# Running the first two groups of a gated-linear-attention + MLP kernel as pairs of units, in the order in which rows and weights land, with x transposed on TensorE and v cast by the software DMA queue

## Chip, cores, metric

One core of a Trainium2 chip (trn2). The metric is the device time of one execution in microseconds, the median of several runs.

## The reference, cut to what matters

```python
# q, k, v, alpha: (B=4, H=8, S=768, D=48), float32
for t in range(S):                      # a gated recurrence, per batch and head
    state = alpha[:, :, t, :, None] * state + einsum('bhd,bhe->bhde', k[:, :, t], v[:, :, t])
    y[:, :, t] = einsum('bhd,bhde->bhe', q[:, :, t], state)
x = y.transpose(0, 2, 1, 3).reshape(3072, 384)
out = gelu_tanh(x @ w_in) @ w_out       # w_in 384 x 2048, w_out 2048 x 384
```

The kernel cuts the sequence into six chunks of 128 rows. A *unit* is one chunk of one batch; a *group* is one chunk of all four batches (four units), a *pair* is two units of a group.

## The kernel before

For each pair: Ln of alpha on ScalarE (`e_ln`), a running sum by a matmul with a triangle (`e_cum`), Exp of it and of its negative and the products with q and k on VectorE (`e_exp`). For each unit: transposes of the scaled q and k on TensorE and their eviction (`t_qk`), the masked scores (`attn`), the new state (`kv`), and the output y, cast to x (`y`). A DMA transpose turns x into xT. Layer 1 then takes a whole group: 16 pieces of 3 matmuls of 512 columns, each with a gelu. Layer 2 has 64 matmuls of 384 columns a group. The *software queue* is that of the DMAs which GpSimd issues, the *hardware queue* that of the DMAs which SyncE issues. A *table load* is ScalarE's exchange of its function tables, which it makes before a Ln, an Exp or a gelu whose set is not loaded (1.28 us each in these traces).

```python
    def load(self, n, group, part=None, cast=False):
        ...
        nc.gpsimd.dma_start(t[:, lo:hi]..., src)              # every load by the software queue
    def cast_v(self, group, part, eng):                       # v of group 0: loaded float32, cast by an engine
        eng(self.loaded["vb", c][:, sl], self.loaded["v", c][:, sl])

    def y(self, cb, xT, i):
        ...
        nc.scalar.copy(x, yps...)
        nc.sync.dma_start_transpose(xT[:, :, i, :], x)        # x to xT by DMA

    def run(self):
        # loads, all from GpSimd: a q k of pair 0, a of pair 1, v of pair 0, q k of pair 1, w_in[0],
        # v of pair 1, w_in[1..3], a q k (by pairs) and v of group 1, w_out[0..3]
        ...
        for i, p in enumerate(pairs[0]):
            ln[i](); cum[i](); exp[i]()
            for cb in p: self.t_qk(cb, nc.scalar.copy)
            self.cast_v(G[0], i, nc.gpsimd.tensor_copy if i == 0 else nc.scalar.copy)
            for cb in p: self.attn(cb)
            for j, cb in enumerate(p): self.yk(cb, xT0, 2 * i + j)
        # then: layer 1 of group 0; Ln, Exp and scores of group 1 with nothing beside them;
        # layer 2 of group g-1 merged with kv, y of group g and Ln, Exp of group g+1;
        # layer 1 of group g merged with the scores of group g+1; and so on to layer 2 of group 5
```

Of the kernel before, what the change touches and what calls it, by code (L numbers as in the profile page):

```python
# [13 lines left out]
DMA_X = True  # L14
# [25 lines left out]
class _Kernel:  # L40
# [41 lines left out]
    def load(self, n, group, part=None, cast=False):  # L82

        nc, C, H, D = self.nc, self.C, self.H, self.D
        c = group[0][0]
        key = (n, c)
        if key not in self.loaded:
            if n == "v" and not cast:
                self.loaded[key] = self.ld.tile([C, len(group), H, D], F32, tag="v32", bufs=1, name="v32")
            else:  # L90
                self.loaded[key] = self.ld.tile([C, len(group), H, D], BF16 if n == "v" else F32, tag=n,
                                                bufs=3 if n == "v" else 2, name=n)
        t = self.loaded[key]
        lo, hi = (0, len(group)) if part is None else (2 * part, 2 * part + 2)
        src = self.src[n][lo:hi].rearrange("b h s d -> s (b h) d")[c * C:(c + 1) * C]
        nc.gpsimd.dma_start(t[:, lo:hi].rearrange("t b h d -> t (b h) d"), src)  # L96
        if n == "v" and cast:
            self.set_v(group, t)
        elif n != "v":
            for i in range(lo, hi, 2):  # L100
                self.u.setdefault(group[i], {})[n + "pair"] = t[:, i:i + 2]

    def set_v(self, group, t):
        for i, cb in enumerate(group):
            self.u.setdefault(cb, {})["v"] = t[:, i]

    def cast_v(self, group, part, eng):
        c = group[0][0]
        if ("vb", c) not in self.loaded:
            t = self.loaded["vb", c] = self.ld.tile([self.C, len(group), self.H, self.D], BF16, tag="v", bufs=3,  # L110
                                                    name="v")
            self.set_v(group, t)
        sl = slice(2 * part, 2 * part + 2)
        eng(self.loaded["vb", c][:, sl], self.loaded["v", c][:, sl])  # L114
# [109 lines left out]
    def y(self, cb, xT, i):  # L224
# [14 lines left out]
        if DMA_X:  # L239
            nc.sync.dma_start_transpose(xT[:, :, i, :], x)  # L240
        else:
            ps = self.ps.tile([C, self.NKT, C], BF16, tag="yk", bufs=2, name="xT_ps")
            for j in range(self.NKT):
                nc.tensor.transpose(ps[:, j, :], x[:, j * C:(j + 1) * C], self.ident)
            nc.vector.tensor_copy(xT[:, :, i, :], ps)
        del self.u[cb]


    def layer1(self, xT, gT):
        nc, C, N = self.nc, self.C, xT.shape[2]  # L250

        def piece(nt):
            h = self.ps.tile([C, N * C], F32, tag="ff", bufs=4, name="hT")
            for j in range(self.NKT):
                nc.tensor.matmul(h, self.w_in[:, j, nt * C:(nt + 1) * C],  # L255
                                 xT[:, j].rearrange("p g t -> p (g t)"),
                                 start=j == 0, stop=j == self.NKT - 1)
            nc.scalar.activation(gT[:, nt, :], h, AF.Gelu_apprx_tanh)  # L258
# [3 lines left out]
    def layer2(self, group, gT, by_part=False):  # L262
# [16 lines left out]
        if by_part:  # L279
            return [lambda mt=mt, part=part: piece(mt, part)  # L280
                    for part in range(self.NFT // 4) for mt in range(len(group))]
        return [lambda mt=mt, part=part: piece(mt, part)
                for mt in range(len(group)) for part in range(self.NFT // 4)]


    def run(self):
# [3 lines left out]
        self.load("a", G[0], 0)  # L290
        make_upper_triangular(nc, self.ut_h, val=1.0, diag=True)
# [5 lines left out]
        self.load("q", G[0], 0)  # L297
        self.load("k", G[0], 0)
        make_identity(nc, self.ident)
        self.load("a", G[0], 1)  # L300
        self.load("v", G[0], 0)
        self.load("q", G[0], 1)
        self.load("k", G[0], 1)
        self.load_w_in(0)
        self.load("v", G[0], 1)
        for i in (1, 2, 3):
            self.load_w_in(i)
        self.load("a", G[1], 0)
        self.load("q", G[1], 0)
        self.load("k", G[1], 0)  # L310
        self.load("a", G[1], 1)
        self.load("q", G[1], 1)
        self.load("k", G[1], 1)
        self.load("v", G[1], cast=True)
        for i in range(4):
            self.load_w_out(i)
        for b in range(self.B):
            for i in range(2):
                nc.vector.memset(self.state[b][i], 0.0)

        def decays(pp):
            return ([lambda p=p: self.e_ln(p) for p in pp],
                    [lambda p=p: self.e_cum(p) for p in pp],
                    [lambda p=p: self.e_exp(p) for p in pp])

        ln, cum, exp = decays(pairs[0])
        xT0 = self.grp.tile([self.C, self.NKT, 4, self.C], BF16, tag="xT", name="xT")
        for i, p in enumerate(pairs[0]):
            ln[i]()
            cum[i]()  # L330
            exp[i]()
            for cb in p:
                self.t_qk(cb, nc.scalar.copy)
# [85 lines left out]
```

## Time and profile before

| | before |
|---|---|
| time, median of the first 3 runs | 253.8 us (253.43 to 255.75) |
| span of the profiled run | 254.0 us |
| busy: TensorE, ScalarE, VectorE, GpSimd | 71%, 47%, 41%, 21% |
| layer 1 of group 0, 1, 2 starts at | 66.7, 115, 144.8 us |

The busy shares are averages over two stages that are limited by different things, so the last row is of more use: a change in the first two groups is worth what it takes from 144.8 us, as long as the steady rest keeps its length. The lines of the profile that carry this stand in the prediction.

In these lines PE is TensorE, PEld its weight loads, ACT ScalarE, DVE VectorE, POOL GpSimd, SP SyncE; L255 is a line of the kernel; hT is the result of layer 1, gT its gelu, acc the sum of layer 2, ot the output tile. A line of the chain of waits gives start, length (us) and what; a line of the list of waits gives the engine that waits, what it waits for, the total, the times and the longest wait. Slices are counted from 0.

### The profile page before, as it was taken

How to read it: one execution, taken by the hardware profiler on the slowest of the kernel's cores; microseconds unless marked ns; L12 is line 12 of the kernel's file. 1: busy time of each engine (PE TensorE's matmuls, PEld its weight loads, DVE VectorE, ACT ScalarE, POOL GpSimd, SP SyncE). 2: the span in 40 equal slices, each digit the busy share in tenths (PEclk: the TensorE clock that was granted, in tenths of full speed). 3: DMA queues.
4: the chain of work that ended last, by engine and by line, in shares of the span. 5: the costliest groups of instructions: out<-in, count | busy, mean ns of one | idle time of the engine just before them, and what ended most of it. 6: DMA issues, size and time to landing. Idle time of an engine off the chain costs nothing.

```text
span 254.0 us, 3728 instructions
## 1 busy us (share of the span) xinstructions
PE 179.4 (71%) x1518; PEld 104.2 (41%) x1528; DVE 105.1 (41%) x203; ACT 119.9 (47%) x188; POOL 52.9 (21%) x48
## 2 busy tenths in 40 slices
PE   0320014500496458999999999989999899998994
PEld 0210013300142334664456555655456545663462
DVE  5340013600000454486558855685567846210011
ACT  2420004420169644456675667647684576316800
POOL 8967264302000261207002340000000000000000
PEclk9999999999999555899999999999999999999999
DMA  4999999999900099995996699222003200131011
GB/s 102 186 185 217 213 186 138 204 213 188 91 0 0 0 194 184 89 161 153 232 51 140 147 184 153 51 68 72 3 0 96 63 34 0 47 106 37 0 65 62
DMA packets 41794, 27.38 MB, mean 108 GB/s; under 512 B 31472, under 2 KB 38128, under 8 KB 41776
## 3 DMA queue, kind: packets, MB, share of 16 engines
q0 software_dynamic: 28336, 20.06, 58.5%
q1 hardware_dynamic: 13440, 7.08, 11.1%
q8 instruction: 12, 0.20, 0.4%
q14 instruction: 6, 0.05, 0.1%
HBM read 25.17 MB, written 4.72 MB: 118 GB/s over the span
## 4 chain that ended last, share of the span: by engine, by line
PE 60%; issue 12%; DVE 9%; DMA 8%; ACT 5%; POOL 4%; DVEq 0%; POOLq 0%; ACTq 0%
PE hT L255 25%; PE acc L270 22%; DMA xT<-x 6%; PE qkT_ps L183 4%; PE at L196 4%; DVE kp L166 2%; ACT qkT L185 2%; PE cum L147 2%; DMA w_in<-in_moe_w_in_dram 2%; DVE qp L164 2%; PE yps L235 2%; DVE st L221 1%; DVE stmp L219 1%; PE yps L232 1%; DVE qkT L185 1%
## 5 line engine op out<-in xcount | busy, mean ns | idle before, releaser
L255 PE MATMUL hT<-xT,w_in 128*128 128x512 bf16 x278 | 70.1, 391 | 18.5 <-DMA xT<-x 16.3
L258 ACT ACTIVATE gT<-hT 128x512 bf16<-128x512 f32 x96 | 57.3, 597 | 41.9 <-PE hT L255 39.0
L270 PE MATMUL acc<-w_out,gT 128*128 128x384 bf16 x384 | 70.2, 333 | 0.0
L255 PEld LDWEIGHTS <-w_in 128*128 128x128 bf16 x288 | 27.0, 100 | 48.3 <-issue 22.3
L270 PEld LDWEIGHTS <-gT 128*128 128x128 bf16 x384 | 35.7, 99 | 22.8 <-issue 2.5
L199 DVE TENSOR_TENSOR atm<-at,ut 128x512 bf16<-128x512 f32 x48 | 30.9, 686 | 24.4 <-PE at L196 24.4
L238 ACT CAST x<-yps 128x384 bf16<-128x384 f32 x24 | 11.5, 478 | 54.3 <-PE yps L235 47.6
L164 DVE TENSOR_TENSOR qp<-q,b 128x768 bf16<-128x768 f32 x12 | 11.5, 959 | 44.6 <-ACT b L160 44.2
L274 DVE COPY ot<-acc 128x384 f32<-128x384 f32 x24 | 13.2, 557 | 34.4 <-PE acc L270 34.3
L96 POOL DMA_DIRECT2D a<-in_alpha_dram x8 | 11.5, 1444 | 56.3 <-ACT la L139 54.5
L210 PE MATMUL kv<-v,kp 128*128 128x96 bf16 x80 | 7.3, 219 | 21.2 <-POOL v L114 20.1
L147 PE MATMUL cum<-la,ut_h 128*128 128x384 f16 x24 | 8.3, 376 | 13.9 <-ACT la L139 13.9
L196 PE MATMUL at<-qkT 64*128 64x128 bf16 x192 | 11.2, 247 | 9.0 <-ACT qkT L185 5.5
L185 DVE COPY qkT<-qkT_ps 128x1024 bf16<-128x1024 bf16 x16 | 11.1, 692 | 13.2 <-PE qkT_ps L183 13.2
L210 PEld LDWEIGHTS <-kp 128*128 128x128 bf16 x80 | 5.8, 103 | 24.4 <-issue 21.6
L96 POOL DMA_DIRECT2D q<-in_q_dram x8 | 11.3, 1419 | 19.8 <-DVE qp L164 18.1
L96 POOL DMA_DIRECT2D v<-in_v_dram x7 | 10.8, 1541 | 18.5 <-issue 18.5
L160 ACT ACTIVATE b<-cum 128x768 bf16<-128x768 f32 x12 | 9.7, 810 | 10.1 <-PE cum L149 7.5
L196 PEld LDWEIGHTS <-qkT 64*128 64x128 bf16 x192 | 6.4, 105 | 18.1 <-ACT qkT L185 7.1
L219 DVE TENSOR_TENSOR stmp<-kv,st 64x192 f32<-64x192 f32 x32 | 11.3, 354 | 6.0 <-PE kv L210 5.6
L183 PE MATMUL qkT_ps<-ident,qp 128*128 128x128 bf16 x96 | 11.1, 249 | 3.8 <-DVE qp L164 3.8
L185 ACT COPY qkT<-qkT_ps 128x1024 bf16<-128x1024 bf16 x8 | 7.9, 1016 | 9.3 <-PE qkT_ps L183 9.3
(37 smaller groups left out, 155.4 us busy)
## 6 DMA issues: line engine op xcount, KB each, us to landing
out_dram<-ot SPq DMA_DIRECT2D x24, 192.0 KB, 1.9
a<-in_alpha_dram POOLq DMA_DIRECT2D x4, 768.0 KB, 7.9
q<-in_q_dram POOLq DMA_DIRECT2D x4, 768.0 KB, 9.3
k<-in_k_dram POOLq DMA_DIRECT2D x4, 768.0 KB, 11.9
v<-in_v_dram POOLq DMA_DIRECT2D x7, 384.0 KB, 11.2
a<-in_alpha_dram POOLq DMA_DIRECT2D x4, 384.0 KB, 10.7
q<-in_q_dram POOLq DMA_DIRECT2D x4, 384.0 KB, 11.8
k<-in_k_dram POOLq DMA_DIRECT2D x4, 384.0 KB, 12.3
```

The costliest lines, as they stand in the source:

```text
L96: nc.gpsimd.dma_start(t[:, lo:hi].rearrange("t b h d -> t (b h) d"), src)
L147: nc.tensor.matmul(cum[:, i, 0:H * D], self.ut_h, la[:, i, :, 0:D], start=True, stop=True)
L164: nc.vector.tensor_tensor(qp[:, :, :, 0:D], u0["qpair"], b8.rearrange("t i (h d) -> t i h d", h=H), op=ALU.mult)
L183: nc.tensor.transpose(ps[:, j, p, :], s[:, 2 * p:2 * p + 2, :].rearrange("t h d -> t (h d)"), self.ident)
L185: (evict or nc.vector.tensor_copy)(t, ps)
L196: nc.tensor.matmul(at[:, o, p, :], kT[sl, p, :], qT[sl, p, :], start=True, stop=True)
L199: nc.vector.tensor_tensor(atm[:, o], at[:, o], self.ut[:, None, :].to_broadcast([C, H // 2, C]), op=ALU.mult)
L219: nc.vector.tensor_tensor(s[ps], acc, old[ps, :, fs], op=ALU.add)
L255: nc.tensor.matmul(h, self.w_in[:, j, nt * C:(nt + 1) * C], xT[:, j].rearrange("p g t -> p (g t)"), start=j == 0, stop=j == self.NKT - 1)
L258: nc.scalar.activation(gT[:, nt, :], h, AF.Gelu_apprx_tanh)
L270: nc.tensor.matmul(acc[mt], gT[:, nt, mt * C:(mt + 1) * C], self.w_out[:, nt, :], start=nt == 0, stop=nt == self.NFT - 1)
L274: nc.vector.tensor_copy(ot, acc[mt])
```

## The change

Its intent: start the matmuls as soon as a pair of units and half of the weights are there. It does five things at once. (1) v of group 0 is cast by the software queue, as for the other groups. (2) x of groups 0 and 1 is transposed on TensorE. (3) Layer 1 of these groups runs by pairs, 256 columns at a time, between the attention stages of the pairs. (4) The loads are ordered to match. (5) alpha of pair 0 goes by the hardware queue (SyncE).

```diff
-        nc.gpsimd.dma_start(t[:, lo:hi].rearrange("t b h d -> t (b h) d"), src)
+        (eng or self.nc.gpsimd).dma_start(t[:, lo:hi].rearrange("t b h d -> t (b h) d"), src)
-    def cast_v(self, group, part, eng):
-        ...
-        if DMA_X:
+        if dma:
             nc.sync.dma_start_transpose(xT[:, :, i, :], x)
+    def t_x(self, cb, xT, i):
+        ps = self.ps.tile([C, self.NKT, C], BF16, tag="yk", bufs=2, name="xT_ps")
+        for j in range(self.NKT):
+            nc.tensor.transpose(ps[:, j, :], self.u[cb]["x"][:, j * C:(j + 1) * C], self.ident)
+        nc.vector.tensor_copy(xT[:, :, i, :], ps)
 ...  (layer1 and layer2 take a range lo:hi of units)
+        self.load("a", G[0], 0, nc.sync)
+        for n in "qkv": self.load(n, G[0], 0)
+        w_in[0..1]; a q k v of pair 1; w_in[2..3]; w_out[0..3]; group 1 by pairs; group 2
 ...
+        ln_exp(p0); scores(p0, copy); state(p0, xT, 0)
+        first = self.layer1(xT, gT, 0, 2)
+        first[:8]
+        self.act_set(LN_EXP_SET)
+        ln_exp(p1); scores(p1, copy); state(p1, xT, 2)
+        first[8:] + self.layer1(xT, gT, 2, 4)
+        self.act_set(LN_EXP_SET)
+        side = [ln_exp(p2)] + scores(p2, copy) + [state(p2, xT1, 0)]
+        _merge(self.layer2(G[0], gT, True), side, 0.5, 1.0)
+        side = [self.act_set(LN_EXP_SET), ln_exp(p3)] + scores(p3)
+        _merge(self.layer1(xT1, gT1, 0, 2), side, 0.7, 1.0)
+        side = [state(p3, xT1, 2)] + [ln_exp(p) for p in pairs[2]]
+        _merge(self.layer2(G[1], gT1, False, 0, 2), side, 0.1, 1.0)
+        side = [f for p in pairs[2] for f in scores(p)]
+        _merge(self.layer1(xT1, gT1, 2, 4), side, 0.1, 1.0)
+        prev = self.layer2(G[1], gT1, False, 2, 4)
+        for g in range(2, len(G)): ...      # as before
```

(The list of loads and the calls are shortened; `lambda`s are left out.)

More of the change, by code (lines that the diff above doesn't have):

```diff
@@ L13 @@
 DMA_QK = False
-DMA_X = True
 def kernel(tc, q, k, v, alpha, moe_w_in, moe_w_out, out):
@@ L80, in pads, with load @@
             self.nc.vector.memset(t[:, :, :, self.D:64], 0.0)
-    def load(self, n, group, part=None, cast=False):
-        nc, C, H, D = self.nc, self.C, self.H, self.D
+    def load(self, n, group, part=None, eng=None):
+        C, H, D = self.C, self.H, self.D
         c = group[0][0]
-        key = (n, c)
-        if key not in self.loaded:
-            if n == "v" and not cast:
-                self.loaded[key] = self.ld.tile([C, len(group), H, D], F32, tag="v32", bufs=1, name="v32")
-            else:
-                self.loaded[key] = self.ld.tile([C, len(group), H, D], BF16 if n == "v" else F32, tag=n,
-                                                bufs=3 if n == "v" else 2, name=n)
-        t = self.loaded[key]
+        if (n, c) not in self.loaded:
+            self.loaded[n, c] = self.ld.tile([C, len(group), H, D], BF16 if n == "v" else F32, tag=n,
+                                             bufs=3 if n == "v" else 2, name=n)
+        t = self.loaded[n, c]
         lo, hi = (0, len(group)) if part is None else (2 * part, 2 * part + 2)
         src = self.src[n][lo:hi].rearrange("b h s d -> s (b h) d")[c * C:(c + 1) * C]
-        nc.gpsimd.dma_start(t[:, lo:hi].rearrange("t b h d -> t (b h) d"), src)
-        if n == "v" and cast:
-            self.set_v(group, t)
-        elif n != "v":
-            for i in range(lo, hi, 2):
-                self.u.setdefault(group[i], {})[n + "pair"] = t[:, i:i + 2]
-    def set_v(self, group, t):
-        for i, cb in enumerate(group):
-            self.u.setdefault(cb, {})["v"] = t[:, i]
-    def cast_v(self, group, part, eng):
-        c = group[0][0]
-        if ("vb", c) not in self.loaded:
-            t = self.loaded["vb", c] = self.ld.tile([self.C, len(group), self.H, self.D], BF16, tag="v", bufs=3,
-                                                    name="v")
-            self.set_v(group, t)
-        sl = slice(2 * part, 2 * part + 2)
-        eng(self.loaded["vb", c][:, sl], self.loaded["v", c][:, sl])
+        (eng or self.nc.gpsimd).dma_start(t[:, lo:hi].rearrange("t b h d -> t (b h) d"), src)
+        for i in range(lo, hi):
+            u = self.u.setdefault(group[i], {})
+            u[n] = t[:, i]
+            if i % 2 == 0:
+                u[n + "pair"] = t[:, i:i + 2]
     def load_w_in(self, part):
@@ L222, in kv, with y @@
                                     u["bend"][ps, :, None].to_broadcast([64, H // 2, D]), op=ALU.mult)
-    def y(self, cb, xT, i):
+    def y(self, cb, xT, i, dma):
         nc, H, C, D = self.nc, self.H, self.C, self.D
@@ L238, in y, with layer1, layer2 @@
         nc.scalar.copy(x, yps.rearrange("t h d -> t (h d)"))
-        if DMA_X:
+        if dma:
             nc.sync.dma_start_transpose(xT[:, :, i, :], x)
-        else:
-            ps = self.ps.tile([C, self.NKT, C], BF16, tag="yk", bufs=2, name="xT_ps")
-            for j in range(self.NKT):
-                nc.tensor.transpose(ps[:, j, :], x[:, j * C:(j + 1) * C], self.ident)
-            nc.vector.tensor_copy(xT[:, :, i, :], ps)
-        del self.u[cb]
-    def layer1(self, xT, gT):
-        nc, C, N = self.nc, self.C, xT.shape[2]
+        u["x"] = x
+    def t_x(self, cb, xT, i):
+        nc, C = self.nc, self.C
+        ps = self.ps.tile([C, self.NKT, C], BF16, tag="yk", bufs=2, name="xT_ps")
+        for j in range(self.NKT):
+            nc.tensor.transpose(ps[:, j, :], self.u[cb]["x"][:, j * C:(j + 1) * C], self.ident)
+        nc.vector.tensor_copy(xT[:, :, i, :], ps)
+    def layer1(self, xT, gT, lo=0, hi=4):
+        nc, C = self.nc, self.C
         def piece(nt):
-            h = self.ps.tile([C, N * C], F32, tag="ff", bufs=4, name="hT")
+            h = self.ps.tile([C, (hi - lo) * C], F32, tag="ff", bufs=4, name="hT")
             for j in range(self.NKT):
                 nc.tensor.matmul(h, self.w_in[:, j, nt * C:(nt + 1) * C],
-                                 xT[:, j].rearrange("p g t -> p (g t)"),
+                                 xT[:, j, lo:hi].rearrange("p g t -> p (g t)"),
                                  start=j == 0, stop=j == self.NKT - 1)
-            nc.scalar.activation(gT[:, nt, :], h, AF.Gelu_apprx_tanh)
+            nc.scalar.activation(gT[:, nt, lo * C:hi * C], h, AF.Gelu_apprx_tanh)
         return [lambda nt=nt: piece(nt) for nt in range(self.NFT)]
-    def layer2(self, group, gT, by_part=False):
+    def layer2(self, group, gT, by_part=False, lo=0, hi=4):
         nc, C = self.nc, self.C
@@ L280, in layer2 @@
             return [lambda mt=mt, part=part: piece(mt, part)
-                    for part in range(self.NFT // 4) for mt in range(len(group))]
+                    for part in range(self.NFT // 4) for mt in range(lo, hi)]
         return [lambda mt=mt, part=part: piece(mt, part)
-                for mt in range(len(group)) for part in range(self.NFT // 4)]
+                for mt in range(lo, hi) for part in range(self.NFT // 4)]
     def run(self):
@@ L289, in run @@
         self.act_set(LN_EXP_SET)
-        self.load("a", G[0], 0)
-        make_upper_triangular(nc, self.ut_h, val=1.0, diag=True)
+        self.load("a", G[0], 0, nc.sync)
+        for n in "qkv":
+            self.load(n, G[0], 0)
+            if n == "q":
+                make_upper_triangular(nc, self.ut_h, val=1.0, diag=True)
+            if n == "k":
+                make_identity(nc, self.ident)
         nc.vector.memset(self.ones, 1.0)
@@ L296, in run @@
         nc.vector.tensor_copy(self.ut, self.ut_h)
-        self.load("q", G[0], 0)
-        self.load("k", G[0], 0)
-        make_identity(nc, self.ident)
-        self.load("a", G[0], 1)
-        self.load("v", G[0], 0)
-        self.load("q", G[0], 1)
-        self.load("k", G[0], 1)
-        self.load_w_in(0)
-        self.load("v", G[0], 1)
-        for i in (1, 2, 3):
-            self.load_w_in(i)
-        self.load("a", G[1], 0)
-        self.load("q", G[1], 0)
-        self.load("k", G[1], 0)
-        self.load("a", G[1], 1)
-        self.load("q", G[1], 1)
-        self.load("k", G[1], 1)
-        self.load("v", G[1], cast=True)
-        for i in range(4):
-            self.load_w_out(i)
         for b in range(self.B):
@@ L319, in run @@
                 nc.vector.memset(self.state[b][i], 0.0)
-        def decays(pp):
-            return ([lambda p=p: self.e_ln(p) for p in pp],
-                    [lambda p=p: self.e_cum(p) for p in pp],
-                    [lambda p=p: self.e_exp(p) for p in pp])
-        ln, cum, exp = decays(pairs[0])
-        xT0 = self.grp.tile([self.C, self.NKT, 4, self.C], BF16, tag="xT", name="xT")
-        for i, p in enumerate(pairs[0]):
-            ln[i]()
-            cum[i]()
-            exp[i]()
-            for cb in p:
-                self.t_qk(cb, nc.scalar.copy)
-            self.cast_v(G[0], i, nc.gpsimd.tensor_copy if i == 0 else nc.scalar.copy)
-            for j, cb in enumerate(p):
-                self.attn(cb)
-            for j, cb in enumerate(p):
-                self.yk(cb, xT0, 2 * i + j)
@@ L340, in run, with ln_exp @@
-        gT_prev = None
-        for g in range(len(G)):
+        for i in range(2):
+            self.load_w_in(i)
+        for n in "aqkv":
+            self.load(n, G[0], 1)
+        for i in range(2, 4):
+            self.load_w_in(i)
+        for i in range(4):
+            self.load_w_out(i)
+        for i in range(2):
+            for n in "aqkv":
+                self.load(n, G[1], i)
+        for n in "aqkv":
+            self.load(n, G[2])
+        def ln_exp(p):
+            self.e_ln(p)
+            self.e_cum(p)
+            self.e_exp(p)
@@ new lines, in scores, with state, new @@
+        def scores(p, evict=None):
+            return [f for cb in p for f in (lambda cb=cb: self.t_qk(cb, evict), lambda cb=cb: self.attn(cb))]
+        def state(p, xT, lo):
+            for i, cb in enumerate(p):
+                self.yk(cb, xT, lo + i, False)
+            for i, cb in enumerate(p):
+                self.t_x(cb, xT, lo + i)
+        def new():
+            return (self.grp.tile([self.C, self.NKT, 4, self.C], BF16, tag="xT", name="xT"),
+                    self.grp.tile([self.C, self.NFT, 4 * self.C], BF16, tag="gT", bufs=1, name="gT"))
@@ new lines, in run @@
+        copy = nc.scalar.copy
+        (p0, p1), (p2, p3) = pairs[0], pairs[1]
+        xT, gT = new()
+        ln_exp(p0)
+        for f in scores(p0, copy):
+            f()
+        state(p0, xT, 0)
+        first = self.layer1(xT, gT, 0, 2)
+        for f in first[:8]:
+            f()
+        self.act_set(LN_EXP_SET)
+        ln_exp(p1)
+        for f in scores(p1, copy):
+            f()
+        state(p1, xT, 2)
+        for f in first[8:] + self.layer1(xT, gT, 2, 4):
+            f()
+        xT1, gT1 = new()
@@ new lines, in run @@
+        self.act_set(LN_EXP_SET)
+        side = [lambda: ln_exp(p2)] + scores(p2, copy) + [lambda: state(p2, xT1, 0)]
+        _merge(self.layer2(G[0], gT, True), side, 0.5, 1.0)
+        side = [lambda: self.act_set(LN_EXP_SET), lambda: ln_exp(p3)] + scores(p3)
+        _merge(self.layer1(xT1, gT1, 0, 2), side, 0.7, 1.0)
+        l2 = self.layer2(G[1], gT1, False, 0, 2)
+        side = [lambda: state(p3, xT1, 2)] + [lambda p=p: ln_exp(p) for p in pairs[2]]
+        _merge(l2, side, 0.1, 1.0)
@@ L342, in run @@
+        side = [f for p in pairs[2] for f in scores(p)]
+        _merge(self.layer1(xT1, gT1, 2, 4), side, 0.1, 1.0)
+        prev = self.layer2(G[1], gT1, False, 2, 4)
+        for g in range(2, len(G)):
             more = g + 1 < len(G)
-            xT = xT0 if g == 0 else self.grp.tile([self.C, self.NKT, 4, self.C], BF16, tag="xT", name="xT")
-            gT = self.grp.tile([self.C, self.NFT, 4 * self.C], BF16, tag="gT", bufs=1, name="gT")
+            xT, gT = new()
             side = []
@@ L347, in run @@
             if more:
-                ln, cum, exp = decays(pairs[g + 1])
-            if g:
-                if g + 2 < len(G):
-                    side.append(lambda: [self.load(n, G[g + 1 + 1], cast=True) for n in "aqkv"])
-                if more:
-                    side += [lambda: self.act_set(LN_EXP_SET), ln[0]]
-                    side += [lambda: self.yk(G[g][0], xT, 0), ln[1]]
-                    side += [lambda: self.yk(G[g][1], xT, 1), cum[0], exp[0]]
-                    side += [lambda: self.yk(G[g][2], xT, 2)]
-                    side += [lambda: self.yk(G[g][3], xT, 3), cum[1], exp[1]]
-                else:
-                    side += [lambda i=i: self.yk(G[g][i], xT, i) for i in range(4)]
-                _merge(self.layer2(G[g - 1], gT_prev, g == 1), side, 0.0, 0.8)
@@ L362, in run @@
-            side = []
-            if g == 0:
-                _merge(self.layer1(xT, gT), side, 0.6, 1.0)
-                self.load("a", G[2])
-                self.act_set(LN_EXP_SET)
-                for i in range(2):
-                    ln[i]()
-                    cum[i]()
-                    exp[i]()
-                for cb in G[1]:
-                    self.t_qk(cb, nc.scalar.copy)
-                    self.attn(cb)
-                for n in "qkv":
-                    self.load(n, G[2], cast=True)
-            else:
-                if more:
-                    for cb in G[g + 1]:
-                        side.append(lambda cb=cb: self.t_qk(cb))
-                        side.append(lambda cb=cb: self.attn(cb))
-                _merge(self.layer1(xT, gT), side, 0.1, 1.0)
@@ L382, in run @@
-            gT_prev = gT
-        for f in self.layer2(G[-1], gT_prev):
+                pp = pairs[g + 1]
+                side.append(lambda: [self.load(n, G[g + 1]) for n in "aqkv"])
+                side += [lambda: self.act_set(LN_EXP_SET), lambda: self.e_ln(pp[0])]
+                side += [lambda: self.yk(G[g][0], xT, 0), lambda: self.e_ln(pp[1])]
+                side += [lambda: self.yk(G[g][1], xT, 1), lambda: self.e_cum(pp[0]), lambda: self.e_exp(pp[0])]
+                side += [lambda: self.yk(G[g][2], xT, 2)]
@@ L384, in run, with yk @@
+                side += [lambda: self.yk(G[g][3], xT, 3), lambda: self.e_cum(pp[1]), lambda: self.e_exp(pp[1])]
+            else:
+                side += [lambda i=i: self.yk(G[g][i], xT, i) for i in range(4)]
+            _merge(prev, side, 0.0, 0.8)
+            side = [f for p in pairs[g + 1] for f in scores(p)] if more else []
+            _merge(self.layer1(xT, gT), side, 0.1, 1.0)
+            prev = self.layer2(G[g], gT)
+        for f in prev:
             f()
-    def yk(self, cb, xT, i):
+    def yk(self, cb, xT, i, dma=True):
@@ L387, in yk @@
         self.kv(cb)
-        self.y(cb, xT, i)
+        self.y(cb, xT, i, dma)
 _INS = ['q', 'k', 'v', 'alpha', 'moe_w_in', 'moe_w_out']
```

## The prediction

> **What bounds the kernel now.** I read the busy slices first, then the chain of waits, then the list of waits, then the timeline of the first 70 us. The slices of the page:
>
> ```profile
> PE   0320014500496458999999999989999899998994
> DMA  4999999999900099995996699222003200131011
> PEclk9999999999999555899999999999999999999999
> ```
>
> A slice is 6.35 us. From slice 16 (102 us) to the end TensorE is full: TensorE bounds the last 150 us. Before that it is nearly empty while the DMA engines are full up to 70 us. The chain of waits, in order of time:
>
> ```profile
> 13.18 4.36 DMA w_in<-in_moe_w_in_dram
> 17.54 19.31 issue
> ...
> 51.02 15.58 DMA xT<-x
> ...
> 67.54 12.52 PE hT L255 x46
> ...
> 98.49 5.01 PE acc L270 x16
> ...
> 144.79 1.67 PE hT L255 x7
> ...
> 230.15 10.09 PE hT L255 x46
> 240.24 10.41 PE acc L270 x64
> ```
>
> So layer 1 of group 0 starts only at 67, its layer 2 at 98, layer 1 of group 2 at 144.8; from there the end is 254.0 - 144.8 = 109.2 us away, and that part is unchanged code. The two gaps have names in the list of waits:
>
> ```profile
> PE kv L210 <- POOL v L114: 20.1, 1, 20.1
> PE hT L255 <- DMA xT<-x: 16.3, 1, 16.3
> ```
>
> and the timeline shows what the first of them is:
>
> ```profile
> 30.34 1.69 POOL L96 DMA_DIRECT2D v<-in_v_dram  x1 [4.99 <-issue]
> 32.02 2.25 POOL L125 DMA_DIRECT2D w_out<-in_moe_w_out_dram  x3
> 34.65 0.74 POOL L125 DMA_DIRECT2D w_out<-in_moe_w_out_dram  x1 [0.38 <-issue]
> 35.39 0.84 POOL L114 CAST v<-v 128x768 bf16<-128x768 f32 x1
> ```
>
> v of pair 0 had landed at 15.4 (the issue that waits for it starts then), but its cast stands behind all load issues in GpSimd's queue, and those wait for room in the software queue. The data of both pairs were in by 23 us, w_in by about 29; compute began 38 us later.
>
> **What the Trainium skill says.** (1) "DMA: Bandwidth & Descriptors", Queues, rings and completion order: each DMA engine goes round-robin between queues, a packet at a time. The trace agrees. In its packet records from 52 to 64 us some 95 transpose packets of 256 B pass in 2 us beside 80 software-queue packets of 4224 B, about 1.2 to 1. Two transposes are 768 packets, 48 per engine; 48/1.2 = 40 turns at 16 x 2/80 = 0.4 us make 16 us, the 15.58 of the chain. (2) Same page, SWDGE vs HWDGE vs iDMA: a casting DMA can only go by GpSimd. The trace has those casts as 96 B packets, 4096 for one group's v in about 4.7 us, against 4.1 us for an uncast group tensor: dearer, but no compute engine is held. (3) "TensorE: Matmul & The Clock Gate", Part 1: the array falls to half clock after an idle window of about 3.4 us. Here the 512-column matmuls of 67 to 72 us start 0.43 us apart, the later ones 10.09/46 = 0.22, and 84 to 103 us is at 0.5. (4) "ScalarE: Activation LUTs", What ACT_TABLE_LOAD costs: about 1283 ns plus a 1380 ns drain. The loads measure 1.283 us, but the Ln after the one at 80.69 starts at 81.99, so no drain is seen here; I use 1.28.
>
> **The change, part by part.** It removes both waits. v comes already cast; x of the first four pairs is transposed on TensorE (three 128x128 transposes and a VectorE copy for each of 8 units, of 24). It reorders: pair 0 complete, half of w_in, pair 1, other half, w_out, groups 1 and 2. It splits layer 1 of groups 0 and 1 into pairs: 64 gelus of 256 columns replace 32 of 512, and 192 matmuls of 256 columns replace 96 of 512. Columns are equal, so warm TensorE time is about equal (0.22/2 = 0.11 each). A gelu is 597 ns at 512 columns and a cast 478 at 384, so 597 - 256 x 0.85 = 0.38 us at 256, against 3 x 0.11 = 0.33 on TensorE: a slight loss, not a bound. It adds table loads: the order of instructions has ten from the Ln of pair 3 to the gelus of that pair, since gelus stand between the Ln/Exp stretches and Ln and Exp get their own sets there.
>
> One hazard: alpha of pair 0 now goes by the hardware queue. Its rows are 192 B, 2048 of them, and output rows of that queue appear as single 1536 B packets, unmerged, where the software queue merges 22 rows into 4224 B. So I expect 2048 small packets, 128 per engine. I guess that 30 of them pass before the software queue starts at 3.5 us; about 14 pass beside q and k (12 packets per engine, 4.4 us); the rest goes packet for packet beside the 128 cast packets of v, some 80 x 0.06 = 5 us. Alpha lands at about 12 us (7 to 15), not 6.4.
>
> Now the start-up chain, from durations of the trace:
> - Alpha 12. From Ln to x in the old pair 1 is 38.9 to 51.0 = 12.1 us; the new order, scores unit by unit and then transposes and copies of x, adds about 2.4: 14.5. xT of pair 0 at 26.5.
> - Eight pieces of layer 1, 24 matmuls at half clock, 24 x 0.21 = 5.1, last gelu 0.4, table load 1.3: Ln of pair 1 at 33.3. Its data are there. xT of pair 1 at 47.8.
> - 72 matmuls, 28 cold in 6 us and 44 x 0.11 = 4.8: 58.6.
> - Layer 2 of group 0: 36 matmuls x 0.163 = 5.9, to 64.5. Then the other 28 lie inside the chain of pair 2, which is again 14.5: 79.
> - Layer 1 of pair 2 with the Ln, Exp and scores of pair 3 beside it: twelve gelus 4.3, then on ScalarE five loads 6.4, Ln 0.85, cum 0.9 (beside a load), exps 1.8, gelus, then the scores: about 17. To 96.
> - Half of layer 2 of group 1 with state of pair 3 (about 4.5) and Ln/Exp of both pairs of group 2, each two loads 2.6, Ln 0.85, cum, exps 1.8, last gelu load 1.3: about 16 until gelus can go on. To 112.
> - Layer 1 of pair 3 with four scores, VectorE 0.69 + 1.29 each, about 2.4 a unit with waits: 9.6, to 122.
> - The other half of layer 2 with the whole state, Ln and Exp stage. The old full stage took 130.0 to 144.4; half its matmuls (5.2 us) go, but VectorE keeps 12.1 - 1.1 = 11 us: about 12, to 134.
> - Cold clock in the sparse stretches of pairs 2 and 3: 48 matmuls at 0.21 instead of 0.11 somewhere on the path, half of that counted, 2 us: 136 with a wide margin, against 144.8 before.
>
> Sum: 136 + 109.2 = 245. Early alpha or better overlap than in my hand-laid chain can only take away, so I say 244. Of the 36 us removed only about 10 remain: the new start has four serial chains of 14.5 us where layer 1 and layer 2 stood idle anyway, and it spends time on tables, on a cold clock and on short stages.
>
> **Rivals.** (a) TensorE bound from 27 us on. For: data are in early, and PE busy is 179 us of 254. If the pair chains hid behind matmuls, removing 36 us would show nearly in full: about 220. Against: the program order puts pair 1's chain after only 24 matmuls, and TensorE is in order, so it waits at each qkT, at and x. (b) Alpha starved. For: the 15.58 us of two transposes beside 4224 B packets; 2048 packets against only such packets would take 2048/95 x 2 = 43 us. Against: the cast packets of v follow q and k closely and let it pass. If it starved until 25 us, everything shifts by 13: 257, slower or same. (c) Loads bound the later pairs. 200 GB/s at the destination gives half a tensor each 2.1 us and a weight quarter each 2.0: w_out in at about 40, group 1 at 57, group 2 at 74, needed at 58, 60 to 80 and about 100. Hidden: 244 stands. Nothing is lost by the longer casts. (d) Table loads and the clock cost more than counted: the stretch 79 to 122 is mostly ScalarE latency, and TensorE at half clock through it adds 6 to 8 us: about 251, within 2%.
>
> **Range and chances.** The step with the greatest doubt is alpha (5 us either way), then the stretch 79 to 122 (6 either way), then the clock (3). Together some 7: 236 to 253. Faster by over 2% is below 248.7; I give it 0.72, within 2% 0.23, slower 0.05 (rival b).
>
> **What will show it.** Right: no wait of kv for a cast, none of hT for xT in the first two groups; alpha's landing near 12 beside 96 B packets; the chain of waits through the first 60 us made of short ACT, DVE and PE pieces and no long DMA piece; ten table loads between 79 and 112; layer 1 of group 2, the first with 512 columns, at about 135, and 109 us from there. Wrong: TensorE busy without holes from 50 us (rival a), a first Ln after 20 us (b), a DMA piece of several us before Ln of pairs 2 to 5 (c), or a tail other than 109 us, which would mean that the change touched the steady part that I hold unchanged.

## The result

| | before | changed |
|---|---|---|
| time, median of 4 runs | 254.15 us (253.43 to 255.75) | 241.84 us (241.28 to 242.51) |
| ratio | | 0.9509, 95% interval 0.9456 to 0.9561 |
| span of the profiled run | 254.0 us | 240.0 us |
| busy: TensorE, ScalarE, VectorE | 71%, 47%, 41% | 78%, 56%, 45% |
| table loads on ScalarE | 11 | 22 |

A ratio is the mean time of one kernel's fast runs over that of the other's fast runs of the same rounds, so not quite the ratio of the medians. The changed kernel is 4.9% faster. The busy slices of the changed kernel (6.0 us each):

```profile
PE   0368258997665387569946999899998999999992
DMA  7999999999900199979999961320012200240011
PEclk9999855999979559999995899999999999999999
```

TensorE now works from slice 2 on, but it is never full for long before slice 22: slices 9 to 17 (54 to 108 us) and 20 and 21 (120 to 132 us) have holes, and the clock row shows half speed at slices 5 and 6, 13 and 14, and again at 21. (The trace has no clock record before 24 us, so the row's first digits say nothing. The first 24 matmuls of layer 1 took 5.09/24 = 0.21 us each for 256 columns, as long as those of 512 columns take at the end.) The chain of waits of the changed kernel (start, length, what):

```profile
3.11 6.22 DMA k<-in_k_dram
...
19.48 5.09 PE hT L239 x24
...
39.25 8.91 PE hT L239 x72
48.16 5.85 PE acc L254 x36
...
61.13 3.81 DMA out_dram<-ot
...
75.17 1.28 ACT L112
76.49 1.26 issue
77.76 0.38 ACT gT L242
78.16 1.28 ACT L121
79.45 0.84 ACT la L121
80.31 1.28 ACT L142
...
119.70 7.85 DMA xT<-x
...
225.31 10.41 PE acc L254 x64
```

The two waits of before are gone and, after the landing of k at 9.3 us, no long DMA piece stands in the first 60 us. At 61.1 us the transfer of an output is on the path, which was not forecast: VectorE waits 1.3 us for it. From 75 us on the path runs through ScalarE's table loads (the pieces named only by a line: L112 by hand, L121, L142 and L242 added automatically before a Ln, an Exp or a gelu; the "issue" at 76.49 is such a load too, which the timeline has at 76.46), and at 119.7 us there is a DMA transpose again, that of group 2, which still goes by DMA. Step by step against the prediction's chain:

| step | predicted us | measured us |
|---|---|---|
| alpha of pair 0 landed, Ln starts | 12.0 | 4.85 |
| chain of pair 0 to xT | 14.5 | 14.6 |
| 24 matmuls, last gelu, table load | 6.8 | 6.8 |
| chain of pair 1 | 14.5 | 13.0 |
| 72 matmuls of layer 1 | 10.8 | 8.9 |
| 36 matmuls of layer 2 | 5.9 | 5.9 |
| chain of pair 2 | 14.5 | 15.3 |
| layer 1 of pair 2, Ln to scores of pair 3 | 17 | 19.9 |
| half of layer 2, state of pair 3, Ln and Exp of group 2 | 16 | 15.6 |
| layer 1 of pair 3 | 9.6 | 8.3 |
| other half of layer 2, state stage of group 2 | 12 | 14.8 |
| allowance for a cold clock | 2 | in the rows above |
| layer 1 of group 2 to the end | 109.2 | 112.0 |
| sum | 244.8 | 240.0 |

The total is close partly because errors cancel: 7 us too many for alpha against 8.5 us too few in three later rows; the other rows together were some 6 us too long. The last of the three is the clock. The stretch of layer 1 of group 2, before and then after (window, length, busy time and count of PE, PEld, DVE, ACT, POOL, then granted clock, DMA share, GB/s):

```profile
144.79:158.51 13.72, 13.53 (x110) 6.92 (x111) 6.96 (x11) 9.28 (x17) 4.40 (x3) 1.00 1.24 159
```

```profile
128.03:144.82 16.79, 16.38 (x111) 8.07 (x114) 6.63 (x10) 9.25 (x16) 1.86 (x2) 0.84 1.09 115
```

The same work takes 3.1 us longer at a mean granted clock of 0.84, just after the wait for xT.

### The profile page after: what moved, and what is told of

It reads as the page before. It is cut to its first block, busy times and chain, and to the rows that moved or that the text cites. A ratio compares the mean times of both kernels' runs of the same rounds, so it can differ in the third digit from the quotient of the medians.

```text
span 240.0 us, 3997 instructions
## 1 busy us (share of the span) xinstructions
PE 186.0 (78%) x1641; PEld 116.0 (48%) x1648; DVE 108.7 (45%) x213; ACT 134.3 (56%) x228; POOL 51.5 (21%) x47
## 4 chain that ended last, share of the span: by engine, by line
PE 59%; DVE 13%; ACT 13%; DMA 7%; issue 5%; POOL 1%; DVEq 0%; POOLq 0%; ACTq 0%
PE hT L239 25%; PE acc L254 21%; PE qkT_ps L165 5%; PE at L178 4%; DMA xT<-x 3%; DVE atm L181 3%; DVE kp L148 3%; DMA k<-in_k_dram 3%; DVE qkT L167 2%; DVE st L203 2%; ACT gT L242 2%; ACT b L142 2%; ACT qkT L167 2%; ACT L142 2%; ACT L121 2%
## 5 line engine op out<-in xcount | busy, mean ns | idle before, releaser
L239 PE MATMUL hT<-xT,w_in 128*128 128x256 bf16 (+1 forms) x377 | 76.3, 352 | 8.1 <-DMA xT<-x 4.2
L242 ACT ACTIVATE gT<-hT 128x256 bf16<-128x256 f32 (+1 forms) x128 | 60.0, 491 | 32.2 <-PE hT L239 30.2
L254 PE MATMUL acc<-w_out,gT 128*128 128x384 bf16 x384 | 68.3, 326 | 0.0
L239 PEld LDWEIGHTS <-w_in 128*128 128x128 bf16 x384 | 38.8, 106 | 33.1 <-issue 6.9
L254 PEld LDWEIGHTS <-gT 128*128 128x128 bf16 x384 | 35.0, 97 | 21.3
L91 POOL DMA_DIRECT2D a<-in_alpha_dram x7 | 10.2, 1458 | 47.1 <-ACT la L121 41.6
L167 DVE COPY qkT<-qkT_ps 128x1024 bf16<-128x1024 bf16 x18 | 12.4, 690 | 16.7 <-PE qkT_ps L165 16.7
L142 ACT ACTIVATE b<-cum 128x768 bf16<-128x768 f32 x12 | 9.7, 811 | 8.9 <-PE cum L131 7.6
L91 POOL DMA_DIRECT2D q<-in_q_dram x8 | 11.5, 1436 | 12.7 <-DVE qp L146 9.2
L91 POOL DMA_DIRECT2D v<-in_v_dram x8 | 11.4, 1428 | 11.1 <-issue 4.7
L165 PEld LDWEIGHTS <-qp 128*128 128x128 bf16 x96 | 7.9, 109 | 11.4 <-DVE qp L146 7.5
L131 PEld LDWEIGHTS <-la 128*128 128x128 f16 x96 | 5.6, 100 | 16.1 <-issue 11.9
L242 ACT ACT_TABLE_LOAD x9 | 11.5, 1283 | 2.5 <-PE hT L239 2.4
L165 PE MATMUL qkT_ps<-ident,kp 128*128 128x128 bf16 x96 | 10.9, 246 | 2.2 <-DVE kp L148 2.2
## 6 DMA issues: line engine op xcount, KB each, us to landing
w_out<-in_moe_w_out_dram POOLq DMA_DIRECT2D x4, 384.0 KB, 14.5
```

Source lines behind the costliest of these rows:

```text
L91: (eng or self.nc.gpsimd).dma_start(t[:, lo:hi].rearrange("t b h d -> t (b h) d"), src)
L142: nc.scalar.activation(b8, cum[:, :, 0:H * D], AF.Exp)
L165: nc.tensor.transpose(ps[:, j, p, :], s[:, 2 * p:2 * p + 2, :].rearrange("t h d -> t (h d)"), self.ident)
L167: (evict or nc.vector.tensor_copy)(t, ps)
L239: nc.tensor.matmul(h, self.w_in[:, j, nt * C:(nt + 1) * C], xT[:, j, lo:hi].rearrange("p g t -> p (g t)"), start=j == 0, stop=j == self.NK ...
L242: nc.scalar.activation(gT[:, nt, lo * C:hi * C], h, AF.Gelu_apprx_tanh)
```

## The experiments

The question left by the result: some 36 us of waits were taken away, and 12 to 14 came out. Theory: the waits are worth nearly their whole length, and the pair order spends most of it again. Rival: the waits would have moved elsewhere anyway, and the pair order is what gains. Eleven kernels were run, all with correct results; none was refused.

| run | what it is | us (median) | ratio to before |
|---|---|---|---|
| changed kernel | | 241.84 | 0.951 |
| e1 | before + v of group 0 cast by the queue | 231.45 | 0.910 |
| e2 | before + x of group 0 on TensorE | 241.14 | 0.948 |
| e3 | before + both | 230.45 | 0.907 |
| e9 | e3 + x of group 1 on TensorE | 223.92 | 0.880 |
| e10 | e9 + half of layer 2 beside the preparation of group 1 | 220.03 | 0.865 |
| e4 | changed, x of groups 0, 1 by DMA | 261.75 | 1.032 |
| e5 | changed, alpha of pair 0 by the software queue | 242.27 | 0.952 |
| e6 | changed, alpha of pair 1 by the hardware queue too | 241.62 (1 run) | |
| e7 | changed, Ln/Exp set loaded once by hand | 236.29 | 0.930 |
| e8 | changed, x of group 2 on TensorE too | 241.97 | 0.951 |
| e11 | pairs for group 0 only | 224.63 | 0.886 |

### e1: the cast alone

```diff
-        self.load("v", G[0], 0)
+        self.load("v", G[0], 0, cast=True)
 ...     (and part 1)
-            self.cast_v(G[0], i, nc.gpsimd.tensor_copy if i == 0 else nc.scalar.copy)
```

> The kernel before with one part of the change: v of group 0 is cast by the software queue; GpSimd's and ScalarE's casts are gone, order and everything else stays. My theory (the two waits are worth nearly their full length, and the pair order then spends most of it): kv of pair 0 starts at about 16 us instead of 36.3, x of pair 1 at about 32 instead of 51, its DMA transposes end between 40 and 47, so layer 1 of group 0 starts 20 to 27 us earlier and the total is about 230 us (226 to 236). Rival 1 (the loads bound the start anyway, the wait only moves): 248 or more. Rival 2 (only both removed together help, because the transpose wait grows by what the cast wait loses): 244 to 250.

Measured 231.45 us (ratio 0.9104, 0.9065 to 0.9144). The matmuls of kv of pair 0 start at 16.1 us. Its chain of waits:

```profile
31.26 11.31 DMA xT<-x
42.71 12.34 PE hT L255 x48
```

Layer 1 of group 0 starts 24 us earlier and the total falls by 22.4. The theory holds, both rivals fall: one of the five parts alone is faster than the whole change by 10 us.

### e2: x on TensorE alone

```diff
-        if DMA_X:
+        if DMA_X and c > 0:
```

> The kernel before with the other part alone: x of group 0 is transposed on TensorE and copied by VectorE, the casts stay. My theory: the cast wait stays (kv at 36.3), xT is ready at about 52.5 instead of 66.7, so the total falls by 12 to 14 us, to about 240. Rival 1 (loads bound): under 3 us less. Rival 2 (the clock or the next group's data take it back): 246 to 250.

Measured 241.14 us (0.9479, 0.9432 to 0.9527). The cast wait stays, the transpose is short:

```profile
17.57 19.33 issue
53.12 13.03 PE hT L255 x48
```

Layer 1 starts 13.6 us earlier, the total falls by 12.7: as the theory said.

### e3: both, without any reordering

The edits of e1 and e2 together.

> The kernel before with both waits removed and nothing else: no pair order, no halved layer 1, no added table loads. My theory: layer 1 of group 0 starts at about 33 to 35 us, nothing later is bound by loads, and the total is 254 - 32 = about 222 us (218 to 229), well below the changed kernel: then the pair order costs about 20 us against this. Rival (the pair order is what gains, because it fills the start): 240 to 250, slower than or equal to the changed kernel.

Measured 230.45 us (0.9065, 0.9025 to 0.9106): above the theory's 222, below the rival's 240. Layer 1 of group 0 does start at 33.0 us. But the chain of waits then shows

```profile
70.81 9.54 DMA xT<-x
81.25 7.33 DMA xT<-x
```

and the list of waits the same thing on two engines:

```profile
PE hT L255 <- DMA xT<-x: 7.7, 2, 7.2
ACT x L238 <- DMA xT<-x: 4.5, 1, 4.5
```

Everything happens earlier now, so the DMA transposes of group 1 meet loads: their packets pass from 75.5 to 87.9 us beside large packets and the 96 B packets of a cast v. In the kernel before they passed at 105.8 to 108.6 and 112.5 to 113.8 us, with few load packets beside them. A gain in the start was turned into a wait one group later. e9 tests this.

### e9 and e10: the same treatment for group 1, and layer 2 in the idle stretch

```diff
-        if DMA_X:
+        if DMA_X and c > 1:                                   # e9
```

```diff
+                l2_0 = self.layer2(G[0], gT, True)            # e10, besides
+                _merge(l2_0[:8], side, 0.0, 1.0)              # side: Ln, Exp, scores of group 1
-                _merge(self.layer2(G[g - 1], gT_prev, g == 1), side, 0.0, 0.8)
+                _merge(l2_0[8:] if g == 1 else self.layer2(G[g - 1], gT_prev), side, 0.0, 0.8)
```

> The kernel before with v of group 0 cast by the software queue and x of groups 0 and 1 transposed on TensorE, so with all that the change does except the order: no pairs, no halved layer 1, loads in the old order. In the run with group 0 alone treated so, layer 1 of group 0 started at 33 us as expected, but layer 1 of group 1 waited for DMA transposes from 81.25 to 88.7. My theory (that wait is what ate the difference to 222): layer 1 of group 1 starts at 81 to 83 and the total is 222 to 225, some 17 to 20 us under the changed kernel, which is then the price of the pair order. Rival (the wait moves on once more, to the transposes of group 2 or to loads of groups 2 and 3): 228 to 231.

> The same, with the first half of layer 2 of group 0 run between the Ln, Exp and scores of group 1, where TensorE otherwise idles for some 18 us, instead of after them. My theory: 8 of its 16 pieces (5.2 us at full clock) leave the path: 3 to 5 us faster than the run without it, 218 to 221. Rival (the following stage is bound by VectorE and ScalarE, so it does not shrink with fewer matmuls): within 1.5 us of it.

e9: 223.92 us (0.8804, 0.8748 to 0.8859). Layer 1 of group 1 starts at 83.5 us. So the wait named in e3 was most of what ate the difference (6.5 of the 8.4 us above 222), and with all that the change does except its order (and alpha's queue) the kernel is 17.9 us faster than the changed one. e10: 220.03 us (0.8645, 0.8599 to 0.8690), 3.9 us below e9. It is the fastest version found. In its chain the rest of layer 2 of group 0 starts at 64.28 us and layer 1 of group 1 at 80.39:

```profile
64.28 1.41 PE acc L270 x8
...
80.39 2.27 PE hT L255 x9
```

### e4: the changed kernel with x by DMA again

```diff
-                self.yk(cb, xT, lo + i, False)
-            for i, cb in enumerate(p):
-                self.t_x(cb, xT, lo + i)
+                self.yk(cb, xT, lo + i, True)
```

> The changed kernel with one part undone: x of the first two groups goes by DMA transposes again. My theory: the transposes of pairs 0 and 1 meet 96 B cast packets and lose 1 to 3 us each, those of pair 2 about 2, those of pair 3 meet 4224 B packets of group 3 and lose up to 6: 246 to 251 in all. Rival (each transpose pair beside loads costs about 15 us as it did before): 265 or more.

Measured 261.75 us (1.0315, 1.0257 to 1.0374), slower than before, above my 246 to 251 and below the rival's 265. The chain of waits:

```profile
18.50 8.12 DMA xT<-x
...
45.80 15.75 DMA xT<-x
```

I had counted 1 to 3 us for pairs 0 and 1, because cast packets of 96 B run near those times. The packet records show that they are over too soon: from 21 to 25 us the transpose packets stand beside packets of w_in of 1024 B, about 150 of each in a microsecond, and from 50 to 60 us beside 4224 B packets, about 57 to 36. So each pair of transposes pays by what the queue happens to carry: 8 us and 16 us here. TensorE's transposes are worth 20 us within this order; without them the changed kernel is slower than the kernel before.

### e5 and e6: alpha by the hardware queue

```diff
-        self.load("a", G[0], 0, nc.sync)      # e5
+        self.load("a", G[0], 0)
```

```diff
         self.load("a", G[0], 0, nc.sync)      # e6
+        self.load("a", G[0], 1, nc.sync)
 ...     (and a of pair 1 is taken out of the later list)
```

> The changed kernel with alpha of pair 0 back at the head of the software queue. The trace of the changed kernel shows it landing at 4.85 us by the hardware queue, not at 12 as I predicted. If the hardware queue helps: Ln starts at 6.5 us, k lands about 1.4 later, and the total rises by 1 to 2 us, to 243 to 244. If my hazard (small hardware packets delayed one for one) had been real: 3 to 7 us faster, 235 to 239.

> Measures the arbitration: alpha of pair 1 goes by the hardware queue too, right behind that of pair 0, so its 2048 packets of 192 B run beside the 4224 B packets of q and k. One packet for one (my prediction's rule): some 14 of its 128 packets per engine pass until q and k are through at 8 us, it ends at about 10 to 12 us, and q and k are not delayed. If the hardware queue passes many descriptors a turn (the trace of the changed kernel has 1212 of them beside 9 software packets between 3 and 4 us): it ends at about 7 us and q, k land about 1.7 us later. Time: 241 to 244 either way.

First the changed kernel, its Ln of pair 0, from the timeline:

```profile
4.85 0.84 ACT L121 ACTIVATE la<-a 128x768 f16<-128x768 f32 x1 [2.83 <-DMA a<-in_alpha_dram]
```

then e5 at the same place:

```profile
6.58 0.84 ACT L121 ACTIVATE la<-a 128x768 f16<-128x768 f32 x1 [4.56 <-DMA a<-in_alpha_dram]
```

The hardware queue brings alpha 1.7 us earlier. By the Ln of pair 1 only 1.0 us of that is left (26.3 against 27.3), and the spans differ by 0.9 (240.0, 240.9). In time, 242.27 us (0.9522, 0.9485 to 0.9560) can't be told from the changed kernel's 0.9509. My hazard would have made e5 faster; for alpha of pair 0 it is refuted. The packet records of the changed kernel say why: 1862 of its 2048 rows had passed before the software queue's first packet started at 3.54 us, and the last started at 3.97. There was hardly anything left to be delayed. (Packet times are on the profile's clock. The 1212 and 9 packets named in the expectation of e6 are from a clock some 0.25 us off; from 3 to 4 us there are 921 and 18.)

e6 shows what such a copy does beside large packets, and it does two things. From 4.0 to 5.5 us 91 rows of 192 B pass beside 67 packets of q, 1.4 to 1, close to one for one; q is not delayed, its last packets pass at about 6 us in both kernels. From 6.0 to 7.4 us 1326 rows pass and no packet of k, though k was issued at 3.11 us in both kernels and its packets pass at that time in the changed one. The last row of alpha of pair 1 passes at about 8.1 us, somewhat later than the 7 I had named for that case, and k pays for it:

```profile
3.11 8.07 DMA k<-in_k_dram
```

against 6.22 in the changed kernel. So this plain copy first shared the engines about evenly and then held the software queue off altogether. What made the difference these runs do not show.

### e7: fewer table loads

```diff
-        side = [lambda: self.act_set(LN_EXP_SET), lambda: ln_exp(p3)] + scores(p3)
+        side = [lambda: (self.act_set(LN_EXP_SET), ln_exp(p3))] + scores(p3)
-        side = [lambda: state(p3, xT1, 2)] + [lambda p=p: ln_exp(p) for p in pairs[2]]
+        side = [lambda: state(p3, xT1, 2), lambda: (self.act_set(LN_EXP_SET), ln_exp(pairs[2][0])),
+                lambda: ln_exp(pairs[2][1])]
```

> The changed kernel with the Ln/Exp set loaded once by hand directly before the Ln of pair 3 and once before those of group 2: six of the ten table loads between 75 and 105 us go (6 x 1.28 = 7.7 us of ScalarE). My theory (that stretch is ScalarE latency on the chain): 5 to 8 us faster, 234 to 237. Rival (VectorE or the clock bounds the stretch): under 2 us faster, 240 to 242.

Measured 236.29 us (0.9298, 0.9259 to 0.9337), 5.5 us below the changed kernel. Where the changed kernel has the chain from 75.17 shown above, this one has

```profile
75.88 1.28 ACT L112
77.17 0.85 ACT la L121
...
78.77 0.82 ACT b L142
```

One load instead of four before the Exp, 22 loads in all become 16. The stretch was ScalarE latency on the path: 5.5 of the 7.7 us removed come out.

### e8: x of group 2 on TensorE

The loop's `yk` for g = 2 is called without DMA and followed by `t_x`.

> The changed kernel with x of group 2 transposed on TensorE as well. Its chain of waits has 7.85 us of DMA transpose at 119.7 us and layer 1 of group 2 after it at half clock. My theory: the wait goes (about 6 us after the cost of 12 transposes and 4 copies) and the cold stretch with it (about 3): 7 to 10 us faster, 232 to 235. Rival (the exposed wait is replaced by the state chain on VectorE): 238 to 241.

Measured 241.97 us (0.9514, 0.9479 to 0.9550): no gain; the theory fell. The DMA wait is gone from its chain, but this came instead:

```profile
126.33 0.50 PE xT_ps L229 x3
...
127.66 2.58 PE acc L254 x8
```

In both traces TensorE does its work in program order. With the DMA transpose only layer 1 waits for it, at the end; with the transpose on TensorE everything behind it in that order waits for x, so the running sums (`cum`) and the last eight matmuls of layer 2 came after 126 us, not at 122, and at half clock (8 in 2.6 us). Layer 1 of group 2 then ends at 144.8 as it did. The rival, that the wait is replaced by the state chain, was right (241.97 is 1 us above its 238 to 241). The cold stretch did not go, it moved: the clock is at half from 124.5 to 131.3 us, from 126.6 to 133.4 in the changed kernel.

### e11: pairs for group 0 only

The changed kernel up to layer 1 of group 0; from there e10's treatment of group 1.

> The changed kernel with pairs for group 0 only: loads, alpha by the hardware queue, casts and the pair order of group 0 as in the change; from layer 2 of group 0 on, group 1 runs as a whole as in the fastest run so far (its preparation inside the first half of layer 2 of group 0, its x on TensorE, its layer 1 with 512 columns, no added table loads). It tells where the price of the pair order sits. If in group 1 (my theory: added table loads, the exposed state chains of pairs 2 and 3, short stages on a cold clock): layer 2 of group 0 starts at 48 us against 45 to 47 in the fastest run, and the total is 220 to 224. If the pair order of group 0 costs as much (its halves of layer 1 on a cold clock): 228 to 236.

Measured 224.63 us (0.8859, 0.8802 to 0.8915), 17.2 below the changed kernel and 4.6 above e10 by the medians (16.5 and 5.4 by the ratios). So, measured against e10, nearly four fifths of the price of the pair order sits in group 1. But e10 and e11 both have layer 2 inside the preparation of group 1, which gained 3.9 us from e9 to e10 and is no part of undoing the order. In group 0 it gains nothing: the table load after layer 1 of group 0 starts at 49.1 us here and at 45.9 in e10, although alpha was in earlier. Part of the 4.6 is again a transpose of group 2:

```profile
109.37 4.17 DMA xT<-x
113.59 2.12 PE hT L239 x9
```

The total is just above the 220 to 224 that I gave for this outcome.

## Why the prediction was right or wrong

**What bounds the kernel: right.** The two waits were real and on the path. e1 and e2 remove one each and get 22.4 and 12.7 us, close to 20.1 and 16.3 us of waiting.

**The total and the direction: right, with cancelling terms.** 241.84 lies in 236 to 253 and near 244.

**Alpha's landing: wrong.** The landing was 4.85 us, not 12. The failing step is "I guess that 30 of them pass before the software queue starts at 3.5 us": 1862 of 2048 rows passed before it, 116 of the 128 of each engine. The next step, "the rest goes packet for packet", is no rule either: the last 186 rows passed beside 16 packets of q, and e6 has 91 rows beside 67 packets, then 1326 beside none. e5 shows that the queue chosen for alpha hardly matters for the time, so it was the size of that term, not the mechanism of the gain, that was wrong.

**Two readings of the prediction were off.** From 52 to 64 us of the kernel before the records hold 502 transpose packets of 256 B beside 494 of 4224 B, so 1.0 to 1 and not 1.2, and the transposes moved packets for 13.2 of the 15.58 us (52.6 to 65.7); that the sum gave 16 us is in part luck. And the 0.85 ns a column of the gelu does not follow from the two times beside it (0.93 would); two copies of the page, 1016 ns at 1024 columns and 478 at 384, give 0.84, and the gelu measured 0.38 us as forecast.

**The chains: right.** 14.5 us a pair was 14.6, 13.0 and 15.3, the last with the 3.81 us transfer of an output in it. The table loads around pair 3 were ten, between 75 and 105 us, as read from the order of instructions (11 more in the whole kernel), and e7 shows that they were on the path.

**The stage of pair 3 (17 us, measured 19.9), the tail stage (12, measured 14.8) and the rest (109.2, measured 112.0): too small.** In the first, TensorE ran at a mean granted clock of 0.68 and the chain walked through five of the stage's six table loads. In the tail stage I let the DMA transposes hide; they were exposed as a 7.85 us piece. The rest was held unchanged, but its first stage began cold. So part of the cold clock that I put down as 2 us on the pairs came out at group 2.

**"Where layer 1 and layer 2 stood idle anyway": wrong as an explanation.** The prediction said that of 36 us only about 10 remain, since the start has serial chains with nothing to do beside them. That made the loss sound unavoidable. e9 has the same kinds of chains without the pair order and keeps 31 us of the 36. The loss is the order's own: 17.9 us against e9, with the order of loads and alpha's queue in it. Against e10, which also hides half of layer 2 (3.9 us), it is 17.2 us in group 1 (e11) and up to 4.6 in group 0. Some 5.5 of it are table loads (e7). The rest I put down to the state chains of pairs 2 and 3, which stand alone on the path, and to half-empty stages at half clock. That split was not measured; e8 shows only that the exposed DMA transpose of group 2 is not the cause by itself.

**Rivals.** (a) "About 220" was nearly reached, but by the kernel that drops the pair order, not by hiding its chains. (b) fell with alpha's landing at 4.85 us. (c), that the loads stay hidden, held: no load stands on the path of pairs 1 to 5 of the changed kernel. (d) was right in kind (e7, the clock).

## What to carry to other kernels

When a profile names two waits, remove each of them alone, and both together, before building a new order around them: here one of the five parts, the cast of v by the software queue, gave 9%, and the whole change with its new order ended at 5%. After a removal look for the same wait one stage later (e3), because work that starts earlier meets transfers that used to be over. When work of two kinds is interleaved on ScalarE, count the table loads that the interleaving adds; and before a transpose moves to TensorE, ask what stands behind it in the program's order (e8).

## What the Trainium skill lacked or had wrong

- "DMA: Bandwidth & Descriptors", Queues, rings and completion order: the page has an engine drain a whole packet, typically some 9 to 17 descriptors, before it turns to the next queue. No one share shows in the records of these runs: for DMA transposes 502 of 256 B beside 494 of 4224 B (kernel before, 52 to 64 us); for a plain copy with 192 B rows 186 beside 16 (changed kernel, 3.54 to 3.97 us), 91 beside 67 and then 1326 beside none (e6). Whether a record of the trace is one descriptor or one packet these runs do not settle.
- Same page, DMA Transpose (X-bar): no word on the latency beside other transfers. The two transposes of a pair took 2.3 us with little beside them (pair 2 of e4), 8.1 and 15.75 us beside loads (pairs 0 and 1).
- Same page, SWDGE vs HWDGE vs iDMA: no rate for a casting load. Half a group's v (393 KB read, 2048 packets of 96 B) took 2.4 us in the changed kernel (7.6 to 10.0 us), as long as the uncast half of q before it (3.5 to 5.9 us), and 2.0 us in e3 (11.1 to 13.1 us).
- "ScalarE: Activation LUTs", What ACT_TABLE_LOAD costs: 1283 ns agrees, but the further 1380 ns of drain do not show. In the changed kernel loads start at 75.17 and 76.46 us, back to back, and the gelu behind the second at 77.76.
